# A gated recurrence with an MLP behind it: the fifth pair's q' and k' turned by the DMA crossbar, and loads that stop for other pairs than before

## The chip, the cores and the metric

One core of a Trainium2 chip runs the whole program. The metric is the device time of one execution in microseconds (us). The kernel before takes 172.65 us (median of three runs, 172.24 to 172.72). One more execution was profiled, and it took 172.37 us. Its span, from the first to the last recorded instruction, is 170.6 us, so 1.8 us lie outside the span.

## The reference

Two parts follow each other. The first is a gated linear recurrence over 4 batches, 8 heads, 768 steps and 48 features; the second is a two-layer MLP with a tanh GELU over all 3072 tokens.

```python
for t in range(S):
    state = alpha[:, :, t, :, None] * state + np.einsum('bhd,bhe->bhde', k[:, :, t], v[:, :, t])
    y[:, :, t] = np.einsum('bhd,bhde->bhe', q[:, :, t], state)
...
x = np.ascontiguousarray(attn_out.transpose(0, 2, 1, 3)).reshape(B * S, H * D)
h = x @ w_in
c = np.float32(np.sqrt(2.0 / np.pi))
g = 0.5 * h * (1.0 + np.tanh(c * (h + 0.044715 * h * h * h)))
return (g @ w_out).astype(np.float32)
```

w_in is 384 x 2048, w_out 2048 x 384. All inputs and the output are float32.

## The kernel before, in words

**Tiles.** The sequence is cut into six chunks of 128 steps. In a chunk the recurrence is done as attention with decays: from alpha come ln(alpha) (`ln`, ScalarE), its running sum (`cum`, a matmul with a triangle of ones), b = exp(sum) and 1/b (`b`, `binv`, ScalarE), and q' = q*b, k' = k/b (`qp`, `kp`, VectorE). Two batches of a chunk make a pair. There are twelve pairs, 0 to 11, so the fifth pair is number 4: pair m belongs to chunk m // 2.

**Turning.** The scores need q' and k' with features on the partitions. For pairs 0 to 4 of the kernel before TensorE turns them (`t`; for pairs 2, 3 and 4 that is `turn_halves`, 32 small transposes into PSUM) and VectorE or ScalarE copies the result to SBUF (`ev`, two copies of 128 x 1024). For the pairs in `TURN_QK` SyncE issues two crossbar DMAs instead (`turn_dma`, L423; `turn5.0` is q' of pair 5, `turn5.1` its k'), which write the turned tile `qkT` with no work on TensorE. In the same way x, the pair's result before the MLP, is turned by TensorE (`tx`, then the copy `xe`), or, for the pairs in `TURN_X`, by one crossbar DMA (`turn_x_dma`, L429; `turn6.2` is that of pair 6).

**The rest of a pair.** `attn` makes the scores and the part of y that comes from the state; `mask` (four on VectorE) zeroes what lies ahead; `y` adds the scores times v; `x` copies y out of PSUM; `kv` and `st` carry the state to the next chunk, with the chunk's last decay row turned by VectorE (`tr`, four per pair).

**The MLP.** A block is two batches of a chunk: `l120.0` to `l120.7` are the first layer of chunk 2, batches 0 and 1 (pair 4's x), six matmuls each; `gelu20.0` to `gelu20.7` follow on ScalarE; `l122` and `gelu22` are batches 2 and 3 (pair 5's x). `l220.0` to `l220.3` are the second layer of chunk 2, batch 0, four matmuls each, `ot20` copies the result out of PSUM, `store20` sends it. ScalarE needs one table for ln and exp and another for GELU; each change loads a table (1.28 us).

**Order.** Nothing is scheduled when the program is built: the list `FIRST` names every step with its engine (P TensorE, V VectorE, A ScalarE, G GpSimd, S SyncE), and each engine runs its own steps in the list's order and waits on semaphores.

**Loads.** q, k, v and alpha of later pairs come by DMAs that GpSimd issues (L246) in the order of `LOADS`. A `gate` (L254) is a one-element copy on GpSimd: it reads a byte of what it names and so holds everything behind it on GpSimd, loads and stores alike, until that has landed. `gate T 5 1` waits for the turned k' of pair 5, `gate X 6 0` for the turned x of pair 6, and from `window 3` on each load is also held until the load three before it has landed. Gates do not stop what is already in the DMA queues. Most stores of results go out from GpSimd too, the others from SyncE.

**Buffers that bind.** PSUM has four `ff` tiles (MLP, half of the scores), two `yk` tiles (turns, y, kv) and one `ca` tile (`cum`, the other half of the scores). Each is handed on when the copy or mask that reads it is done.

Of the kernel before, what the change touches and what calls it, by code (L numbers as in the profile page):

```python
# [76 lines left out]
class _Kernel:  # L77
# [5 lines left out]
             "aqkv 3", "aqkv 4", "aqkv 5", "aqk 6", "a 7", "gate T 5 1", "q 7", "a 8", "k 7", "v 6", "window 3", "v 7", "qkv 8", "gate T 6 0", "aq 9", "gate X 6 0", "kv 9", "aqkv 10", "a 11", "gate X 8 0", "qkv 11")  # L83
# [22 lines left out]
        P:l110.1 A:gelu10.5 V:ev3.0 A:ev3.1 P:kv2.1 P:l110.7 A:gelu10.3 A:gelu10.1 A:gelu10.7 P:kv3.0 V:tr3.2 V:tr3.3 V:st2.1 P:l110.4 A:gelu10.4
        P:l110.2 A:gelu10.2 P:l211.0 G:load.a7.0 V:st3.0 P:attn3.0 V:mask3.2 V:mask3.3 P:l211.1 P:l211.2 A:ln4.0 P:cum4.0 A:b4.0 V:mask3.0 V:mask3.1
        V:qp4.0 P:l210.0 P:y3.0 P:l211.3 A:x3.0 P:y3.1 P:kv3.1 A:binv4.0 P:l210.1 P:l210.2 V:st3.1 V:tr4.0 A:x3.1 A:ln5.0 P:tx3.1 V:xe3.1 A:ot11.0
        P:tx3.0 V:xe3.0 V:tr4.1 P:cum5.0 G:store02.0 A:b5.0 S:store03.0 P:l210.3 P:l112.0 P:l112.7 S:store11.0 A:ot10.0 A:binv5.0 V:kp4.0 V:qp5.0
        S:turn5.0 V:kp5.0 S:turn5.1 G:gate.T5.1 G:load.q7.0 G:load.a8.0 G:load.k7.0 G:load.v6.0 G:gate.a8.0 G:load.v7.0 A:gelu12.0 A:gelu12.7 P:t4.0  # L110
        V:ev4.0 P:l112.3 P:l112.5 V:ev4.1 V:tr4.2 V:tr4.3 P:l112.4 P:kv4.0 V:st4.0 A:gelu12.3 A:gelu12.5 A:gelu12.4 P:l112.6 A:gelu12.6 S:store01.0
        P:l112.1 P:l112.2 A:gelu12.1 V:tr5.0 P:attn4.0 A:gelu12.2 P:l212.0 P:l212.1 V:mask4.2 V:mask4.0 V:mask4.1 P:l212.2 P:y4.0 P:l212.3 V:mask4.3
        P:y4.1 A:ln6.0 P:cum6.0 A:x4.0 P:l213.0 V:tr5.1 A:ot12.0 A:x4.1 P:tx4.0 V:xe4.0 A:binv6.0 P:tx4.1 V:xe4.1 V:kp6.0 P:l213.1 A:b6.0 P:l213.2
        P:kv4.1 V:st4.1 P:l213.3 A:ln7.0 V:ot13.0 P:l120.0 P:attn5.0 V:mask5.0 V:mask5.1 V:mask5.2 V:mask5.3 V:tr6.0 V:tr6.2 V:tr6.1 P:l120.2 V:tr5.2
        V:tr5.3 A:gelu20.0 A:gelu20.2 P:l120.6 P:l120.7 A:gelu20.6 P:l120.1 A:gelu20.1 P:y5.0 V:x5.0 P:l120.4 A:gelu20.7 A:gelu20.4 P:l120.5 P:l120.3
        A:gelu20.5 V:qp6.0 V:tr6.3 G:gate.k7.0 G:load.q8.0 G:gate.v6.0 G:load.k8.0 S:turn6.1 A:gelu20.3 P:cum7.0 P:y5.1 V:x5.1 P:l221.0 P:kv5.0
        P:l220.0 P:tx5.1 P:l221.1 V:st5.0 G:gate.v7.0 G:load.v8.0 V:xe5.1 A:b7.0 P:l220.1 P:tx5.0 V:qp7.0 V:xe5.0 S:turn6.0 G:gate.T6.0 G:gate.q8.0
        G:load.a9.0 P:l221.2 P:kv5.1 A:binv7.0 S:turn7.0 V:st5.1 A:ln8.0 P:cum8.0 A:binv8.0 A:b8.0 P:l221.3 P:l220.2 P:l220.3 A:ot21.0 P:attn6.0
        V:kp7.0 A:ot20.0 P:l122.0 P:l122.2 G:store21.0 V:mask6.0 V:mask6.1 V:mask6.2 V:mask6.3 P:l122.7 A:gelu22.0 A:gelu22.2 P:l122.4 V:tr7.0 V:tr7.1
        G:store13.0 G:store12.0 P:y6.0 A:gelu22.4 A:gelu22.7 P:l122.1 P:y6.1 A:gelu22.1 A:x6.0 P:l122.6 V:x6.1 P:l122.3 G:store10.0 P:kv6.1 V:st6.1  # L120
        P:l122.5 P:kv6.0 V:st6.0 P:l223.0 A:gelu22.3 P:l223.1 A:gelu22.6 A:gelu22.5 P:l223.2 S:turn7.1 G:store20.0 S:turn6.2 G:gate.k8.0 V:qp8.0
# [22 lines left out]
    """.split()  # L144
    ACROSS, GAP = (0, 1), 112

    TURN_QK, TURN_X = (5, 6, 7, 8, 9, 10, 11), (6, 7, 8, 9, 10, 11)

    XPK = 48
    INTER = (2, 3, 4, 5, 6, 7, 8, 9, 10, 11)  # L150
# [9 lines left out]
                a=5, q=5, k=5, vb=5)  # L160
# [713 lines left out]
```

## Time and profile before

| | |
|---|---|
| median of three runs | 172.65 us (172.24 to 172.72) |
| profiled execution | 172.37 us, of it span 170.6 us |
| TensorE busy | 164.7 us (97%) |
| ScalarE busy | 127.0 us (74%) |
| VectorE busy | 105.5 us (62%) |
| GpSimd busy | 73.2 us (43%) |
| read from and written to memory | 25.17 MB and 4.72 MB |

How to read it: a matmul's record covers its way through the array, so that a busy TensorE overlaps itself. What a matmul costs is read from the distance between starts, which the chain of waits gives. Crossbar DMAs and loads are busy neither on SyncE nor on an engine; their cost is the time from issue to landing, and who waits for the landing. The row of a gate on GpSimd shows how long loads stood still.

### The profile page before, as it was taken

Reading aid. Unit: us, or ns where it says so; the run is one execution under the profiler, and the core shown is the slowest. Engines: PE = TensorE matmul, PEld = TensorE weight load, DVE = VectorE, ACT = ScalarE, POOL = GpSimd, SP = SyncE. Lnnn points to the kernel's source line nnn. Section 1 sums busy time; section 2 is a strip of 40 time slices with the busy share of each in tenths; the row PEclk is TensorE's granted clock in tenths of the full one; section 3 lists DMA queues with packets and bytes.
Section 4 is the critical chain, followed back from the end, with each engine's and each line's share of the span. In section 5 each row is a group of like instructions: output and inputs, shape, how many; then the busy total and the mean of one; then the engine's idle time right before and its main releaser. Section 6 shows DMA issues by size and latency. Waiting matters only on the chain.

```text
span 170.6 us, 4706 instructions
## 1 busy us (share of the span) xinstructions
PE 164.7 (97%) x1965; PEld 130.3 (76%) x1966; DVE 105.5 (62%) x201; ACT 127.0 (74%) x207; POOL 73.2 (43%) x100
## 2 busy tenths in 40 slices
PE   7799999999999999999999999999999999999993
PEld 2478899666886797796697697796796795986973
DVE  6499512478978997799877957765953740620000
ACT  3687688897998998969788399587978783453741
POOL 6488346996565003753990267350800600100000
PEclk9999999999999999999999999999999999999999
DMA  4999999999999995899999999999397595121104
GB/s 132 303 215 158 224 252 253 223 218 217 262 212 192 218 210 140 205 168 181 194 230 306 151 137 130 190 197 258 85 180 169 81 176 124 50 53 39 50 0 140
DMA packets 56389, 29.53 MB, mean 173 GB/s; under 512 B 45840, under 2 KB 52432, under 8 KB 56368
## 3 DMA queue, kind: packets, MB, share of 16 engines
q0 software_dynamic: 31216, 19.67, 71.0%
q1 hardware_dynamic: 24608, 9.18, 29.7%
q10 hardware_dynamic: 544, 0.39, 0.8%
q8 instruction: 15, 0.25, 0.6%
q14 instruction: 6, 0.05, 0.1%
HBM read 25.17 MB, written 4.72 MB: 175 GB/s over the span
## 4 chain that ended last, share of the span: by engine, by line
PE 81%; DMA 7%; DVE 4%; ACT 3%; SPq 2%; issue 1%; POOL 1%; POOLq 0%
PE hT L558 34%; PE acc L577 33%; DMA wide<-in_v_dram 4%; PE at L447 3%; DMA k<-in_k_dram 3%; PE yps L526 2%; PE cum L318 2%; PE kv L476 2%; DVE tr L490 2%; SPq L243 2%; DVE atm L466 1%; ACT qkT L386 1%; PE yps L456 1%; PE xT_ps L545 1%; PE xT_ps L516 1%
## 5 line engine op out<-in xcount | busy, mean ns | idle before, releaser
L558 PE MATMUL hT<-xT,w_in 128*128 128x256 bf16 (+1 forms) x672 | 69.9, 258 | 0.0
L577 PE MATMUL acc<-w_out,gT 128*128 128x384 bf16 (+3 forms) x416 | 68.6, 314 | 0.0
L564 ACT ACTIVATE gT<-hT 128x512 bf16<-128x512 f32 x96 | 52.6, 602 | 15.0 <-PE hT L558 13.9
L558 PEld LDWEIGHTS <-w_in 128*128 128x128 bf16 x672 | 61.9, 113 | 1.4
L577 PEld LDWEIGHTS <-gT 128*128 128x128 bf16 x416 | 37.3, 98 | 20.3
L466 DVE TENSOR_TENSOR atm<-at,ut 128x512 bf16<-128x512 f32 x48 | 30.2, 683 | 4.9 <-PE at L447 4.9
L589 DVE COPY ot<-acc 128x384 f32<-128x384 f32 (+1 forms) x7 | 3.6, 509 | 25.8 <-PE acc L577 25.6
L589 ACT COPY ot<-acc 128x384 f32<-128x384 f32 (+2 forms) x19 | 8.8, 461 | 13.4 <-PE acc L577 9.6
L602 POOL DMA_DIRECT2D out_dram<-ot x14 | 7.7, 553 | 19.9 <-DVE ot L589 19.7
L355 DVE TENSOR_TENSOR kp<-k,binv 128x768 bf16<-128x768 f32 (+1 forms) x15 | 11.9, 795 | 4.9 <-DMA k<-in_k_dram 2.2
L490 DVE STREAM_TRANSPOSE tr<-b 32x256 f32<-32x256 f32 x32 | 14.0, 439 | 0.8
L246 POOL DMA_DIRECT2D q<-in_q_dram x11 | 12.3, 1115 | 4.6 <-DMA w_in<-in_moe_w_in_dram 2.2
L246 POOL DMA_DIRECT2D a<-in_alpha_dram x11 | 12.2, 1110 | 4.2 <-issue 1.1
L218 ACT ACT_TABLE_LOAD x10 | 12.8, 1283 | 0.9 <-PEq L858 0.7
L246 POOL DMA_DIRECT2D k<-in_k_dram x11 | 12.2, 1113 | 2.8 <-issue 1.2
L501 DVE TENSOR_TENSOR stmp<-kv,st 128x384 f32<-128x384 f32 x16 | 8.9, 557 | 7.2 <-PE kv L476 6.5
L246 POOL DMA_DIRECT2D vb<-in_v_dram x11 | 12.2, 1108 | 2.3 <-issue 0.6
L564 ACT ACT_TABLE_LOAD x10 | 12.8, 1283 | 0.2
L355 DVE TENSOR_TENSOR qp<-q,b 128x768 bf16<-128x768 f32 (+1 forms) x15 | 11.9, 795 | 1.4 <-ACT b L344 1.2
L344 ACT ACTIVATE b<-cum 128x768 f32<-128x768 f32 (+1 forms) x15 | 10.1, 684 | 2.5 <-PE cum L318 1.5
L344 ACT ACTIVATE binv<-cum 128x768 bf16<-128x768 f32 (+1 forms) x15 | 10.3, 689 | 1.6 <-PE cum L318 1.4
L503 DVE TENSOR_TENSOR st<-stmp,tr 128x384 bf16<-128x384 f32 x16 | 8.9, 558 | 0.6
(77 smaller groups left out, 149.0 us busy)
## 6 DMA issues: line engine op xcount, KB each, us to landing
a<-in_alpha_dram POOLq DMA_DIRECT2D x9, 384.0 KB, 9.0
q<-in_q_dram POOLq DMA_DIRECT2D x9, 384.0 KB, 8.0
k<-in_k_dram POOLq DMA_DIRECT2D x9, 384.0 KB, 8.0
out_dram<-ot POOLq DMA_DIRECT2D x10, 192.0 KB, 6.3
vb<-in_v_dram POOLq DMA_DIRECT2D x9, 192.0 KB, 8.0
out_dram<-ot SPq DMA_DIRECT2D x9, 192.0 KB, 2.4
w_in<-in_moe_w_in_dram POOLq DMA_DIRECT2D x4, 384.0 KB, 8.5
w_out<-in_moe_w_out_dram POOLq DMA_DIRECT2D x4, 384.0 KB, 10.5
```

Of the source, the lines that this page charges most:

```text
L218: nc.scalar.add_instruction(mybir.InstLoadActFuncSet(name=nc.get_next_instruction_name(), act_func_set_id=i, engine=mybir.EngineType.Activ ...
L246: dma(u[t][:, lo:hi].rearrange("t b h d -> t (b h) d"), src.rearrange("b h s d -> s (b h) d")[c * C:(c + 1) * C])
L344: self.nc.scalar.activation(u[n].rearrange("t i h d -> t i (h d)")[:, lo:hi], cum, AF.Exp, scale=1.0 if n == "b" else -1.0)
L355: self.nc.vector.tensor_tensor(out, rows, b, op=ALU.mult)
L466: self.nc.vector.tensor_tensor(u["atm", i][:, o], u["at", i][o], self.ut[:, None, :].to_broadcast([self.C, self.H // 2, self.C]), op=ALU.mult)
L490: self.nc.vector.transpose(u["tr"][f:f + 32, :, 0:32], rows[:, lo:lo + H * 2 * D].rearrange("t (g n) -> t g n", n=2 * D)[:, :, 0:32])
L501: nc.vector.tensor_tensor(s, acc, old, op=ALU.add)
L503: nc.vector.tensor_tensor(new, acc, end[:, :, None].to_broadcast([C, H // 2, 2 * D]), op=ALU.mult)
L558: self.nc.tensor.matmul(h[:, s].rearrange("p (g t) -> p g t", t=self.C), w_in[:, j, nt % 4 + s], self.xT[c % self.NX][:, lo:hi, j], start= ...
L564: return lambda e: self.nc.scalar.activation(self.gT[c % self.NG][:, nt:nt + 4 // (hi - lo), lo * self.C:hi * self.C], f.pop(("h", c, lo, ...
L577: self.nc.tensor.matmul(f["acc", c, b][:, lo:hi], self.gT[c % self.NG][:, nt, b * self.C:(b + 1) * self.C], self.w_out[:, nt, lo:hi], star ...
L589: self.copy(e)(f["ot", c, b][:, sl], f["acc", c, b] if half is None else f["acc", c, b, half][:, sl])
```

## The change

`TURN_QK` gets pair 4, so that its q' and k' are turned by two crossbar DMAs (`turn4.1`, `turn4.0`). TensorE's `t4.0` (32 transposes) and the two copies `ev4.0` and `ev4.1` on VectorE go.

`LOADS` gets other gates and another order. Before there were T5 (k'), T6 (q'), X6 and X8. Now there are T4 (q'), T5 (q' and k'), T7 (q' and k'), X6 and X8: no gate for the turned q' of pair 6, two more stops for pairs 4 and 7.

`FIRST` is written anew. On each engine the order is the same as before up to the start of chunk 1's MLP (about 45 us into the span) and again from `l142` on (about 134 us); between, it differs on all five engines. No step other than those named is added or removed.

```diff
     LOADS = ("gate a 0 1", "v 0", "gate k 0 1", "in 0", "v 1", "in 1", "in 2", "in 3", "out 0", "out 1", "aqk 2 a", "out 2", "aqk 2 b", "out 3", "v 2",
-             "aqkv 3", "aqkv 4", "aqkv 5", "aqk 6", "a 7", "gate T 5 1", "q 7", "a 8", "k 7", "v 6", "window 3", "v 7", "qkv 8", "gate T 6 0", "aq 9", "gate X 6 0", "kv 9", "aqkv 10", "a 11", "gate X 8 0", "qkv 11")
+             "aqkv 3", "aqkv 4", "aqk 5", "a 6", "gate T 4 0", "k 6", "a 7", "q 6", "gate T 5 0", "gate T 5 1", "v 5", "q 7", "a 8", "k 7", "v 6", "window 3", "v 7", "q 8", "a 9", "gate T 7 0", "gate T 7 1", "gate X 6 0", "kv 8", "qkv 9", "aqkv 10", "a 11", "gate X 8 0", "qkv 11")
...
-        G:load.q9.0 G:gate.X6.0 P:l222.0 V:tr7.2 V:tr7.3 V:kp8.0 P:l222.1 S:turn8.0 P:attn7.0 V:mask7.2 V:mask7.3 P:l223.3 A:ln9.0 P:l222.2 P:l222.3
...
+        P:attn7.0 A:gelu22.1 A:gelu22.3 G:store21.0 G:store13.0 G:store12.0 G:store10.0 G:store20.0 S:turn6.2 G:gate.X6.0 G:gate.v7.0 G:load.k8.0
...
-    TURN_QK, TURN_X = (5, 6, 7, 8, 9, 10, 11), (6, 7, 8, 9, 10, 11)
+    TURN_QK, TURN_X = (4, 5, 6, 7, 8, 9, 10, 11), (6, 7, 8, 9, 10, 11)
```

GpSimd, from the load of pair 8's q to the gate X6 (`gate<-xT_103`), before the change. `gate<-qkT` is the gate T6, the other gates are those of the window; the loads of k and vb are pair 8's, those of a and of the second q pair 9's:

```order
L246 DMA q<-in_q_dram 128x16x48
L254 CAST gate<-vb 128x1
L246 DMA k<-in_k_dram 128x16x48
L254 CAST gate<-vb 128x1
L246 DMA vb<-in_v_dram 128x16x48
L254 CAST gate<-qkT 128x1
L254 COPY gate<-q 128x1
L246 DMA a<-in_alpha_dram 128x16x48
L602 DMA out_dram<-ot 128x384 x5
L254 COPY gate<-k 128x1
L246 DMA q<-in_q_dram 128x16x48
L254 CAST gate<-xT_103 128x1
```

The same engine from the load of pair 8's q on in the changed kernel. `gate<-qkT 128x1 x2` are the two gates T7, and k, vb and the second q behind `gate<-xT_103` are pair 8's k and v and pair 9's q:

```order
L247 DMA q<-in_q_dram 128x16x48
L255 CAST gate<-vb 128x1
L247 DMA a<-in_alpha_dram 128x16x48
L255 CAST gate<-qkT 128x1 x2
L603 DMA out_dram<-ot 128x384 x5
L255 CAST gate<-xT_103 128x1
L255 CAST gate<-vb 128x1
L247 DMA k<-in_k_dram 128x16x48
L255 COPY gate<-q 128x1
L247 DMA vb<-in_v_dram 128x16x48
L255 COPY gate<-a 128x1
L247 DMA q<-in_q_dram 128x16x48
```

Pair 8's k and v have moved from ahead of the five stores to behind them and behind the gate X6.

SyncE, from its first store to the turned q' of pair 7, in the changed kernel (`kp_95` and `qp_91` are k' and q' of pair 4; the rows behind the three stores are pairs 5, 6 and 7):

```order
L603 DMA out_dram<-ot 128x384
L424 DMA_TRANSPOSE qkT<-kp_95 128x8x128
L424 DMA_TRANSPOSE qkT<-qp_91 128x8x128
L603 DMA out_dram<-ot 128x384 x3
L424 DMA_TRANSPOSE qkT<-qp_92 128x8x128
L424 DMA_TRANSPOSE qkT<-kp_96 128x8x128
L424 DMA_TRANSPOSE qkT<-kp_97 128x8x128
L424 DMA_TRANSPOSE qkT<-qp_93 128x8x128
L424 DMA_TRANSPOSE qkT<-kp_98 128x8x128
L424 DMA_TRANSPOSE qkT<-qp_94 128x8x128
```

Before, the rows of `kp_95` and `qp_91` were not there, and the first crossbar DMA was pair 5's; now three stores and pair 5's two turns stand behind pair 4's two.

VectorE, from q' of pair 8 (`qp_91`), which stands behind the first of pair 7's four masks, to its k' (`kp_95`), in the changed kernel; `atm` are the other three masks, `tr` decay rows, `ot` the result of chunk 2's batch 3, the two `x` are pair 7's:

```order
L356 TENSOR_TENSOR qp_91<-q,b_99 128x16x48
L491 STREAM_TRANSPOSE tr<-b_100 32x8x32
L467 TENSOR_TENSOR atm<-at,ut 128x512
L491 STREAM_TRANSPOSE tr<-b_99 32x8x32
L467 TENSOR_TENSOR atm<-at,ut 128x512 x2
L590 COPY ot<-acc 128x384
L491 STREAM_TRANSPOSE tr<-b_99 32x8x32
L537 CAST x<-yps 128x8x48
L491 STREAM_TRANSPOSE tr<-b_99 32x8x32
L537 CAST x<-yps 128x8x48
L356 TENSOR_TENSOR kp_95<-k,binv 128x16x48
```

Before, k' of pair 8 stood ahead of the four masks of pair 7. On TensorE `l130.1`, a first user of pair 6's turned x, now stands one second-layer step behind `attn7.0`; before, `l130.0` was the first, three second-layer steps and `cum9.0` behind `attn7.0`.

More of the change, by code (lines that the diff above doesn't have):

```diff
@@ L106 @@
[L106 to L113, printed above, removed]
@@ L118 @@
[L118 to L121, printed above, removed]
```

95 lines of the change are left out of this document (54 added, 41 removed).

## The prediction, on record before the changed kernel ran

> **What bounds the kernel now.** I began with the page: busy times, the granted clock, the shares of the chain of waits.
>
> ```profile
> span 170.6 us, 4706 instructions
> ...
> PE 164.7 (97%) x1965; PEld 130.3 (76%) x1966; DVE 105.5 (62%) x201; ACT 127.0 (74%) x207; POOL 73.2 (43%) x100
> ...
> PEclk9999999999999999999999999999999999999999
> DMA  4999999999999995899999999999397595121104
> ...
> PE 81%; DMA 7%; DVE 4%; ACT 3%; SPq 2%; issue 1%; POOL 1%; POOLq 0%
> ```
>
> TensorE is the bound, at a full granted clock. The DMA engines are also occupied nearly throughout up to three quarters of the span, so whatever is added there must share. Then the chain of waits in order of time, which has what each step of TensorE costs:
>
> ```profile
> 59.05 0.57 PE qkT_ps L379 x32
> ...
> 63.98 0.55 PE at L447 x16
> 64.53 0.20 PE yps L456 x16
> ...
> 66.79 0.20 PE yps L526 x8
> 66.99 0.65 PE acc L577 x4
> ...
> 67.84 0.33 PE cum L318 x2
> ...
> 70.45 0.17 PE kv L476 x4
> 70.62 0.65 PE acc L577 x4
> 71.27 0.65 PE hT L558 x6
> ```
>
> A step of either MLP layer costs 0.65 us, the scores 0.75, a `y` 0.20, a `cum` 0.33, a `kv` 0.17. From 45 us to the end these fill TensorE almost without a hole, and what stands in the list behind 134 us is the same in both kernels. So only two things can move the end: work that leaves TensorE, and waits of TensorE that go or come between 45 and 134 us.
>
> **What goes.** `t4.0` takes 0.57 us (first row above); with the 0.1 us that TensorE loses when it turns to 64-row matmuls (60 us less the step ahead of it, below) that is **0.67 us**.
>
> ```profile
> 51.27 1.48 PE L577 MATMUL acc<-w_out,gT 128*128 128x384 bf16 x8
> 52.77 0.48 PE L318 MATMUL cum<-la,ut_h 128*128 128x384 f16 x2
> ...
> 57.58 1.47 PE L558 MATMUL hT<-xT,w_in 128*128 128x256 bf16 x12
> 58.98 0.41 PE L379 MATMUL qkT_ps<-ident,qp 64*128 64x64 bf16 x16
> ...
> 78.78 0.81 PE L577 MATMUL acc<-w_out,gT 128*128 128x384 bf16 x4
> 79.76 0.34 PE L545 MATMUL xT_ps<-ident,x 128*128 128x128 bf16 x3 [0.16 <-DVE x L536]
> ```
>
> Two steps from 57.58 would end at 58.88, and the transposes start at 58.98: the 0.1 us. The same subtraction gives the waits that stand there now: 52.77 - 51.27 - 1.30 = 0.20 us ahead of pair 4's `cum`, and 79.76 - 78.78 - 0.65 = 0.33 us ahead of pair 5's `tx`. In the new order one step of the MLP more stands ahead of `cum4.0`, and `x5.1` is read 2.6 us later, behind four second-layer steps, so I let both go: **0.53 us**. VectorE is also rid of two copies (0.69 us each, as another pair's copy below shows); it is not the bound, so this counts only through the waits.
>
> ```profile
> 46.23 0.69 DVE L386 COPY qkT<-qkT_ps 128x1024 bf16<-128x1024 bf16 x1
> ...
> 64.02 0.60 ACT L564 ACTIVATE gT<-hT 128x512 bf16<-128x512 f32 x1
> 64.63 1.28 ACT L218 ACT_TABLE_LOAD   x1
> 65.93 0.84 ACT L301 ACTIVATE la<-a 128x768 f16<-128x768 f32 x1
> ...
> 84.59 0.62 PE L447 MATMUL at<-qkT 64*128 64x128 bf16 x16
> ...
> 85.02 2.48 DVE L466 TENSOR_TENSOR atm<-at,ut 128x512 bf16<-128x512 f32 x4 [0.58 <-PE at L447]
> ...
> 89.25 0.56 DVE L536 CAST x<-yps 128x384 bf16<-128x384 f32 x1 [0.82 <-PE yps L526]
> ...
> 94.98 0.96 DVE L355 TENSOR_TENSOR kp<-k,binv 128x768 bf16<-128x768 f32 x1
> ```
>
> **Short waits that come.** Positions in the new order come from the step costs above, laid along the new list from 45 us on. Pair 4's scores begin at 63.4 (63.98 less `t4.0`'s 0.67, less the 0.20, plus a wait of 0.2 below and small change). With TensorE that much ahead, ScalarE's pace shows. The last GELU of `l112` ends about 64.3 (64.62 in its row, 0.3 earlier now), then the table (1.28) and ln of pair 6 (0.84) end at 66.5; `cum6.0` is due at 66.3 (scores 63.4 + 0.75, three steps, one `y`): 0.2. In the same way `cum8.0` waits 0.1, `l211.0` 0.2 (on ScalarE the copy `ev3.0` stands ahead of `gelu10.1`). The masks of pair 6 stand behind three small VectorE steps and end 0.3 after `y6.1` is due; `ot23.0` behind pair 7's masks frees its PSUM tile 0.25 late for `l130.3`; `y8.1` waits 0.1. Together **1.2 us**. None of these exists in the trace of before; each is a handover that I know to about 0.2 us, so the sum lies between 0.3 and 2.0.
>
> **What the added crossbar DMAs cost.** First the microseconds from issue to landing: of all turned q' and k', of `turn6.2` (answer for 90 to 91 us), of pair 9's k and pair 8's k' (97 to 99 us), and the median of GpSimd's stores. Then the issues on SyncE and GpSimd, a gate, and the first user of `turn6.2` on TensorE, in the timeline:
>
> ```profile
> DMA to landing us min/median/max: 2.7/5.6/7.7
> ...
> xT<-x SPq DMA_TRANSPOSE x1, 6.5
> ...
> k<-in_k_dram POOLq DMA_DIRECT2D x1, 384.0 KB, 5.7
> ...
> qkT<-kp SPq DMA_TRANSPOSE x1, 2.7
> ...
> out_dram<-ot POOLq DMA_DIRECT2D x10, 192.0 KB, 6.3
> ```
>
> ```profile
> 90.16 2.10 SPq L429 DMA_TRANSPOSE xT<-x  x1
> ...
> 79.05 1.16 POOL L246 DMA_DIRECT2D k<-in_k_dram  x1 [0.37 <-DVE qp L355]
> ...
> 85.58 2.71 POOL L602 DMA_DIRECT2D out_dram<-ot  x5
> ...
> 96.74 0.18 POOL L254 CAST gate<-xT 128x1 f32<-128x1 bf16 x1 [7.16 <-DMA xT<-x]
> ...
> 97.37 1.17 POOL L246 DMA_DIRECT2D k<-in_k_dram  x1 [0.19 <-issue]
> ...
> 97.75 0.82 PE L558 MATMUL hT<-xT,w_in 128*128 128x256 bf16 x6
> ```
>
> A turned q' or k' takes 2.7 to 7.7 us to land; the shortest is pair 8's k', issued while GpSimd stood still (the 7.16 us in front of X6). For pair 4 the new writes are issued at about 55.0 and 56.5 (k' and q' behind pair 3's masks) and read at 63.4: 6.9 us for the later one. With the loads stopped behind pair 6's alpha I take no wait; without that cover it is at most 0.8 (7.7 - 6.9). Pair 5's are read at 71, pair 6's q' is issued at 76.5 and read at 84.4: 7.9 us, no wait. Behind pair 5's gate stands pair 5's v, needed at 75.0; the gate opens at about 65, so it lands in time. The three stores that now stand behind pair 4's turns on SyncE keep nobody waiting.
>
> The price lies between the scores of pairs 6 and 8. **First, x of pair 6.** VectorE ended its masks 0.43 + 2.48 = 2.9 us after the start of `attn6.0`; three small steps stand ahead of them now, so 3.2. Two copies of 0.56 follow, and `turn6.2` is issued at 4.35. TensorE has until `l130.1` eight steps of `l122`, two `y`, two `kv`, `attn7.0` and `l223.0`, with the scores at the start 0.75 + 5.24 + 0.41 + 0.34 + 0.85 + 0.65, and the wait of 0.3 above: 8.55. So 4.2 us are left, where before it was 97.75 - 90.16 = 7.6 us, and the write took 6.5 of them. Alone it takes about 3 (pair 8's 2.7); but the five stores, freed when pair 7's gate opens (its second write issued at 84.3, behind `kp7.0`, so about 87.5), go out in the same microseconds, as they did before (85.58 on), and loads do not. I take 4.8, between: a wait of **0.6**, bounds 0 (2.7) and 2.3 (6.5).
>
> **Second, k' of pair 8.** Its load was issued at 79.05; now it stands behind X6. From the issue of `turn6.2`: landing 4.8, gate and issue 0.6 (96.74 to 97.37), load 5.7, `kp8.0` 1.0: `turn8.1` is issued at 12.1. The loads behind are running again, so I take 6.2 to land, in the upper half of the row: 18.3. TensorE needs from `l130.1` to the scores of pair 8 eight first-layer and ten second-layer steps, two `y`, a `cum`, two `kv` and the short wait: 13.1, so 4.8 + 13.1 = 17.9. A wait of **0.4**, bounds 0 and 3.0 (if both writes take longest). VectorE is not held for it: behind `kp8.0` stands `st7.1`, whose `kv` comes later. Pair 9's loads start some 3 us later than before, and are read that much later too.
>
> **Sum.** -0.67 - 0.53 + 1.2 + 0.6 + 0.4 = +1.0 us. The profiled execution took 172.37 us (span 170.6 and 1.8 around it), so 173.4; the median of the runs shown is 0.28 above that execution, which gives **173.6 us**.
>
> [...]
>
> **Rivals.**
>
> *The stops do what they can, and TensorE is never kept.* Place: the 4.2 us of `turn6.2` and the 5.8 left for `turn8.1`. For it speaks that pair 8's k', with GpSimd held, took 2.7 us, and that VectorE starts 1.4 us lighter. Both waits are then 0, and if the short waits are half of my sum the result is -1.2 + 0.6 = -0.6: **172.0 us**, faster. It decides at 4.2 us for `turn6.2`.
>
> *The stores hold x.* The stop for pair 7 releases five stores immediately ahead of `turn6.2`; such stores land 6.3 us after issue (last row). If the turned x lands only with the last of them, at 87.5 + 2.7 + 6.3 = 96.5, against 92.9 due, TensorE waits 3.6 and k of pair 8 follows later still: 173.6 + 3.0 = **176.6 us**. Against it: SyncE's queue is another one than GpSimd's. [...]
>
> *Pair 4's turns are late.* The loads ahead of T4 are still in the queues, and with 7.7 us and a second delay on pair 5's gate `attn4.0` and `y5.0` wait together some 2 us: **175.5 us**. For it: the loads that are in the queues there took 11 to 12 us to land (answer for 44 to 53.5 us, pair 5's and 6's k).
>
> ```profile
> k<-in_k_dram POOLq DMA_DIRECT2D x2, 384.0 KB, 11.8
> ```
>
> *Given back exactly:* one of the two waits, fewer short ones, within 0.3% of before, about **172.7 us**.
>
> **How the numbers follow.** Forecast (0.3 to 2.2 us above before) 0.45; never kept 0.22; stores hold x 0.13; pair 4 late 0.08; given back 0.12. A measurement of this kernel tells about 0.3% (0.5 us) from no change. Faster by more than that: most of the second case, 0.19. Within: the last case, the rest of the second and the lower end of the forecast, 0.21. Slower: 0.60. The range goes from 171.6 (172.65 - 1.2 + short waits of 0.3, and 0.15 for the scatter of runs) to 176.2, which leaves out most of the stores' case and a tail below.
>
> **What would show it.** In the changed profile: 32 matmuls of L379 fewer, and no hole in TensorE at 52.8 and 79.8; a hole in TensorE ahead of the first `hT` behind the seventh scores, ended by the DMA of x, and one ahead of pair 8's scores, ended by the DMA of k'; the gate X6 opening at 93 to 95; the loads of pair 8's k landing near 100. If TensorE has no hole there, the waits were wrong; if holes stand before 80 us, pair 4 or 5 was late; if the short waits in front of the `cum` steps are absent, ScalarE was not as close behind as I say.

## The result, and the profile after

The changed kernel takes **176.7 us** (median of five runs, 175.9 to 177.75); the kernel before took 172.33 us beside it (five runs, 171.81 to 172.72). The ratio is 1.0258, with a 95% interval from 1.0211 to 1.0305. The prediction had the sign right and the size wrong: +4.4 us where it said +1.0, and outside its range. The profiled execution of the changed kernel took 176.54 us, of it span 174.7. (Medians here are over all runs of a kernel; ratios leave disturbed runs out, so the two need not match exactly.)

First the page of the changed kernel: the span, TensorE, the DMA engines by slices of 4.37 us, the chain by engine, k' on VectorE, and the gates on turned q' and k'.

```profile
span 174.7 us, 4655 instructions
...
PE 165.2 (95%) x1933; PEld 130.4 (75%) x1934; DVE 105.6 (60%) x202; ACT 126.5 (72%) x204; POOL 74.9 (43%) x105
...
DMA  4999999999994889999994999999994494121104
...
PE 63%; DMA 23%; ACT 5%; POOL 4%; issue 2%; SPq 1%; DVE 1%; POOLq 0%; ACTq 0%
...
L356 DVE TENSOR_TENSOR kp<-k,binv 128x768 bf16<-128x768 f32 (+1 forms) x15 | 11.9, 795 | 6.5 <-DMA k<-in_k_dram 5.3
...
L255 POOL CAST gate<-qkT 128x1 f32<-128x1 bf16 x5 | 1.6, 323 | 26.5 <-DMA qkT<-qp 24.0
```

TensorE is as busy as before; what is new is that the chain runs 23% of the span through DMAs (7% before) and that VectorE waits 5.3 us for k (2.2 before). The row of the DMA engines has two slices at 4 that were full before, from 52 to 57 us and from 92 to 96 us: there the loads stood still at a gate. GpSimd waited 26.5 us in front of turned q' and k' (12.2 before).

Then TensorE in the timeline (start, duration, step; the bracket is the idle time before the row), at the places that the prediction named:

```profile
51.73 1.47 PE L578 MATMUL acc<-w_out,gT 128*128 128x384 bf16 x8
53.24 0.48 PE L319 MATMUL cum<-la,ut_h 128*128 128x384 f16 x2
...
66.41 0.36 PE L527 MATMUL yps<-vb,atm 128*128 128x48 bf16 x8
66.77 0.48 PE L319 MATMUL cum<-la,ut_h 128*128 128x384 f16 x2
...
81.19 0.81 PE L578 MATMUL acc<-w_out,gT 128*128 128x384 bf16 x4
81.99 0.48 PE L319 MATMUL cum<-la,ut_h 128*128 128x384 f16 x2
...
90.30 1.25 PE L559 MATMUL hT<-xT,w_in 128*128 128x256 bf16 x10
92.25 0.62 PE L448 MATMUL at<-qkT 64*128 64x128 bf16 x16 [0.70 <-ACT gT L565]
...
93.66 0.82 PE L559 MATMUL hT<-xT,w_in 128*128 128x256 bf16 x6
...
104.20 2.44 PE L578 MATMUL acc<-w_out,gT 128*128 128x384 bf16 x14
109.26 0.62 PE L448 MATMUL at<-qkT 64*128 64x128 bf16 x16 [2.62 <-DMA qkT<-kp]
```

Distances between starts give the holes, as in the prediction: ten first-layer matmuls at 0.109 us end at 91.39 and pair 7's scores start at 92.25, a hole of 0.86; fourteen second-layer matmuls at 0.163 end at 106.48 and pair 8's scores start at 109.26, a hole of 2.78. (The bracket shows 0.16 us less each time: a matmul's record is that much longer than the distance between starts, 0.273 us against 0.109 in the first layer, 0.326 against 0.163 in the second.) Of each hole 0.10 us is not new: TensorE lost that ahead of these scores in the kernel before too (109.06 - 103.76 - 5.20 for pair 8, with 5.20 for 32 second-layer matmuls). `cum4.0` still waits 0.20, `cum6.0` 0.16, `cum8.0` 0.15; `y6.1` waits 0.24, a first-layer step at 128.8 waits 0.33, and `kv3.0` at 49.41 now waits 0.17. The bracket at 92.25 names a GELU, but that is not who was waited for: in the experiment e7 the same GELU ends at 92.39 and the scores stand at 91.69. Pair 7's turned q' landed at 92.11, as the chain shows.

The chain of waits of the changed kernel from 84 to 110 us (start, duration, what):

```profile
84.50 7.61 DMA qkT<-qp
...
92.48 0.18 POOL gate L255
...
93.04 1.38 POOL out_dram L603 x3
...
95.77 0.20 POOL gate L255
...
96.39 6.44 DMA k<-in_k_dram
...
102.85 0.96 DVE kp L356
...
103.84 5.38 DMA qkT<-kp
...
109.26 0.62 PE at L448 x16
```

These eight rows carry most of the loss. Pair 7's q' takes 7.61 us to land. Until then its gate holds GpSimd, behind it five stores have to be issued, then comes the gate X6 (no wait any more), and only at 96.39 the load of pair 8's k; 6.44 later VectorE makes k', 5.38 after that it is turned, and TensorE, which asked at 106.48, goes on at 109.26.

The stops that stand ahead of all this are those for pairs 4 and 5, in GpSimd's timeline of the changed kernel:

```profile
61.62 0.18 POOL L255 CAST gate<-qkT 128x1 f32<-128x1 bf16 x1 [15.09 <-DMA qkT<-qp]
...
68.40 0.86 POOL L255 CAST gate<-qkT 128x1 f32<-128x1 bf16 x1 [2.45 <-DMA qkT<-kp]
```

They hold the loads for 15.1 and 2.5 us, and v of pair 7 is issued at 79.5. In the kernel before the one stop here held them for 12.0 us, and v of pair 7 went out at 74.1.

The account closes. At `l142.0`, behind which both lists are the same, the changed kernel is 3.76 us later. The profiled run was 0.30 later already at pair 2's scores (37.81 against 37.51), where the lists are still the same. Then -0.67 (`t4.0`), -0.33 (pair 5's `tx`), +0.17 (`kv3.0`), +0.55 (`cum6.0`, `cum8.0`, `y6.1`), +0.76 and +2.68 (the two holes less their 0.10 each) and +0.33 make 3.79.

### The profile page after: what moved, and what is told of

Same layout as the page of the kernel before. It is cut to its first block, busy times and chain, and to the rows that moved or that the text cites. A ratio compares the mean times of both kernels' runs of the same rounds, so it can differ in the third digit from the quotient of the medians.

```text
span 174.7 us, 4655 instructions
## 1 busy us (share of the span) xinstructions
PE 165.2 (95%) x1933; PEld 130.4 (75%) x1934; DVE 105.6 (60%) x202; ACT 126.5 (72%) x204; POOL 74.9 (43%) x105
## 4 chain that ended last, share of the span: by engine, by line
PE 63%; DMA 23%; ACT 5%; POOL 4%; issue 2%; SPq 1%; DVE 1%; POOLq 0%; ACTq 0%
PE acc L578 26%; PE hT L559 26%; DMA k<-in_k_dram 7%; DMA qkT<-qp 4%; DMA wide<-in_v_dram 4%; DMA out_dram<-ot 4%; DMA qkT<-kp 3%; PE at L448 2%; PE cum L319 2%; PE yps L527 2%; PE kv L477 2%; POOL out_dram L603 2%; SPq L244 1%; ACT L565 1%; ACT qkT L387 1%
## 5 line engine op out<-in xcount | busy, mean ns | idle before, releaser
L590 ACT COPY ot<-acc 128x384 f32<-128x384 f32 (+2 forms) x18 | 8.3, 459 | 14.3 <-PE acc L578 9.3
L603 POOL DMA_DIRECT2D out_dram<-ot x16 | 8.8, 554 | 21.2 <-DVE ot L590 19.3
L247 POOL DMA_DIRECT2D a<-in_alpha_dram x11 | 12.2, 1111 | 3.9 <-issue 1.6
L247 POOL DMA_DIRECT2D q<-in_q_dram x11 | 12.2, 1112 | 2.2 <-DMA w_in<-in_moe_w_in_dram 1.0
L247 POOL DMA_DIRECT2D vb<-in_v_dram x11 | 12.2, 1111 | 2.2 <-DMA w_out<-in_moe_w_out_dram 1.1
L255 POOL CAST gate<-qkT 128x1 f32<-128x1 bf16 x5 | 1.6, 323 | 26.5 <-DMA qkT<-qp 24.0
```

The source lines that it names most:

```text
L247: dma(u[t][:, lo:hi].rearrange("t b h d -> t (b h) d"), src.rearrange("b h s d -> s (b h) d")[c * C:(c + 1) * C])
L590: self.copy(e)(f["ot", c, b][:, sl], f["acc", c, b] if half is None else f["acc", c, b, half][:, sl])
L603: return lambda e: (self.nc.sync if e == "SP" else self.nc.gpsimd).dma_start(self.out[r:r + self.C, sl], f["ot", c, b][:, sl])
```

## The experiments

Each kernel was timed against the kernel before on the same chip, which took 172.04 to 172.18 us there. The first theory, from the trace above, was **L**: what the stops take from the loads makes later loads land late, and TensorE waits where its list meets them. Its narrow form is that only pair 8's k, behind pair 7's stop, is late. The rival **S**: the crossbar's own writes are slow whatever the loads do.

### e1: is the late k of pair 8 the loss?

```diff
+            mine = self.p[3, 1] if (u["m"], n) == (8, "k") else u
-            out, rows, b = u[n + "p"][:, lo:hi, :, 0:self.D], u[n][:, lo:hi], u["b" if n == "q" else "binv"][:, lo:hi]
+            out, rows, b = u[n + "p"][:, lo:hi, :, 0:self.D], mine[n][:, lo:hi], u["b" if n == "q" else "binv"][:, lo:hi]
```

> The changed kernel, but k' of pair 8 is made from pair 7's k, which is long there; pair 8's k is still loaded and never read, so the result is not the reference's. Theory 'late load': the 2.8 us hole of TensorE ahead of pair 8's scores is the late k of pair 8. VectorE then makes k' at about 100.4 instead of 102.9, the crossbar write is issued about 2.5 us earlier, the hole shrinks to 0.3 to 0.5, and the time falls by about 2.3 us, to about 174.4. Rival 'slow write': the hole is the crossbar write's own length among running loads; it starts earlier, meets more loads, still lands near 109, and the time stays within 0.7 us of 176.7.

Measured: 176.72 us, ratio 1.0244 (1.0187 to 1.0301), no gain. TensorE of e1 in the timeline:

```profile
92.07 0.62 PE L448 MATMUL at<-qkT 64*128 64x128 bf16 x16 [1.31 <-DMA qkT<-qp]
107.73 0.62 PE L448 MATMUL at<-qkT 64*128 64x128 bf16 x16 [1.27 <-DMA qkT<-kp]
126.91 2.12 PE L559 MATMUL hT<-xT,w_in 128*128 128x256 bf16 x18 [1.77 <-ACT ot L590]
129.56 0.81 PE L559 MATMUL hT<-xT,w_in 128*128 128x256 bf16 x6 [0.53 <-ACT gT L565]
```

k' of pair 8 was made at 100.2 instead of 102.85 and the hole ahead of pair 8's scores halved, but the one ahead of pair 7's scores grew to 1.48, and new ones opened in chunk 4's first layer. There ScalarE's copy of a result (`ot`) had waited 2.76 us for an earlier store to land (126.28), and the matmuls wait for what ScalarE does then; the 0.33 of the change at 128.8 has the same cause (a store that lands at 125.51). The narrow form falls: without the late k the time stays, and the waits stand elsewhere.

### e2, e3: one stop fewer

e2 takes `gate T 4 0` out of `LOADS`, e3 both `gate T 7`; nothing else.

> The changed kernel without the gate on the turned q' of pair 4: GpSimd goes on loading k, alpha, q at 47 us instead of 62. Theory 'lost load time': the 15 us during which GpSimd stood still put every later load about 4 us behind the old order; without this stop q, alpha, k of pairs 7 and 8 land 3 to 4 us earlier, the loads ahead of pair 7's stop have drained when its crossbar writes are issued, that stop opens at about 88 instead of 92, k of pair 8 lands at about 98, and both holes (0.9 and 2.8 us) go: about 173.3. Against it stands that pair 4's own crossbar writes then share with loads and land 2 to 4 us later than at 61.6, against 63.7 due: up to 2 us are lost there, so 173.3 to 175. Theory 'late load' alone, with pair 7's stop as the cause, leaves the stop opening above 91 and the time within 0.7 us of 176.7.

Measured: 177.74 us, ratio 1.0292 (1.0222 to 1.0363). TensorE of e2 in the timeline (of a run of 181.31 us, the longest of four):

```profile
64.52 0.62 PE L447 MATMUL at<-qkT 64*128 64x128 bf16 x16 [1.95 <-DMA qkT<-qp]
94.91 0.62 PE L447 MATMUL at<-qkT 64*128 64x128 bf16 x16 [1.05 <-DMA qkT<-qp]
112.38 0.62 PE L447 MATMUL at<-qkT 64*128 64x128 bf16 x16 [3.07 <-DMA qkT<-kp]
```

Without the stop pair 4's turned q' itself comes late, and the two later holes stay. No load time came back: pair 5's turns stand behind pair 4's on SyncE, GpSimd stood 15.6 us at pair 5's gate instead, and v of pair 7 went out at 80.4. So e2 does not test the lost load time. It does show that, once pair 4 goes by the crossbar, pair 4's own scores wait if its stop is taken out.

> The changed kernel without the two gates on pair 7. Theory 'late load': GpSimd issues the five stores at 83 instead of 93 and then stands at the gate on x of pair 6, whose write is now slower (stores beside it): it lands at 94 to 96, k of pair 8 is issued at about the same time as now (96.4) or 1.5 us earlier; the hole ahead of pair 8's scores shrinks by no more than 1.5 us, and one of 1 to 2 us opens ahead of the first user of x: 175.5 to 177.5. Rival 'pair 7's stop is the whole cost': with it gone the time returns to 173 to 174.

Measured: 177.33 us, ratio 1.0203 (1.0146 to 1.0259). TensorE of e3 in the timeline:

```profile
92.14 0.62 PE L447 MATMUL at<-qkT 64*128 64x128 bf16 x16 [0.48 <-DMA qkT<-qp]
94.60 0.85 PE L558 MATMUL hT<-xT,w_in 128*128 128x256 bf16 x6 [0.89 <-DMA xT<-x]
108.74 0.62 PE L447 MATMUL at<-qkT 64*128 64x128 bf16 x16 [1.13 <-DMA qkT<-kp]
```

The hole at pair 8 shrinks, x of pair 6 is now late for `l130.1`. The interval overlaps the change's: no verdict between the two on the time, only on the places. The rival's 173 to 174 us falls: by the ratio it is 175.5.

### e4: pair 4 by the crossbar in the kernel before

Only `TURN_QK` with pair 4 and `turn4.0`, `turn4.1` behind `kp4.0`; no new stop, no new order.

> The kernel before with one part of the change alone: q' and k' of pair 4 go by the crossbar, directly behind k' of pair 4 on SyncE's list; no gate, no load and no other step is moved. Theory: the two writes meet a queue with 11 us of loads, land not before 65, and TensorE waits 1.5 to 3 us ahead of pair 4's scores, less the 0.7 that leave it: 173.3 to 174.8. If a crossbar write is as quick among loads as alone (3 to 4 us), it lands by 63 and the time is 171.7 to 172.2.

Measured: 176.63 us, ratio 1.018 (1.0092 to 1.0267). Pair 4's turn is late by 2.44 us at 65.58, and that hole has an after-effect (under e8). Taking 0.67 us of transposes off TensorE costs more than it brings here too.

### e5: no loads from pair 8 on

```diff
+            if u["m"] > 7:
+                u[t] = self.p[3, 1][t]
+                return
```

> The changed kernel without the loads of a, q, k and v of pairs 8 to 11: their tiles stand for pair 7's, so part of the output is computed from pair 7's inputs; every stop, transpose, matmul and store stays. Theory L (the stops take load time out of DMA queues that were nearly always busy, so that the loads of pairs 7 to 11 land 5 to 17 us later and TensorE meets them): nothing of pairs 8 to 11 is late any more, turn8.1 is issued near 95 and takes under 4 us, the holes ahead of attn7 (0.86 us), attn8 (2.78 us) and l140.2 (0.33 us) go, and the time is 172.0 to 173.2 us. Rival S (the crossbar writes themselves, 5 to 8 us each, are what is late, whatever the loads do): turn7.0 and turn8.1 still take 5 us and more, at least 2 us of the holes stay, and the time is 175 us or more.

Measured: 175.12 us (173.28 to 176.24), ratio 1.0138 (1.0027 to 1.0248): the median is S's number, the interval also holds L's. The places speak against S: turn7.0 landed in 2.8 us and turn8.1 in 3.4, and the holes ahead of both scores went. But another came, 2.2 us ahead of `l130.1`, in TensorE's timeline of e5:

```profile
94.64 1.47 PE L561 MATMUL hT<-xT,w_in 128*128 128x256 bf16 x6 [2.06 <-DMA xT<-x]
```

Pair 7's gate opened at 86.90, so the five stores went out beside `turn6.2`, which took 6.3 us. That looks like the prediction's rival "the stores hold x", seen here once. In e7, with the gate at 87.80, it took 3.7 us beside the same five stores and nothing waited. Two of the stores were issued ahead of it in e5 (6.3 us), one in e7 and e10 (3.7 and 4.3), none in e9 (2.7), which fits the rival. No run varies the stores alone, so the cause is not shown.

### e6: the old loads from pair 7 on, behind the stops for pairs 4 and 5

```diff
-... "v 7", "q 8", "a 9", "gate T 7 0", "gate T 7 1", "gate X 6 0", "kv 8", "qkv 9", ...
+... "v 7", "qkv 8", "gate T 6 0", "aq 9", "gate X 6 0", "kv 9", ...
```

> The changed kernel with the kernel before's list of loads from v of pair 7 on: no stop for pair 7, k and v of pair 8 ahead of a of pair 9, the stop for q' of pair 6 back; the stops for pairs 4 and 5 and everything else stay. Theory L: k of pair 8 is issued near 84 and lands near 90 (5 us behind the kernel before, 12 us ahead of the change), kp8 near 96 to 98, the hole ahead of attn8 falls under 1 us, but what the stops for pairs 4 and 5 took is still missing, so that 1 to 2 us of waits show elsewhere: 173.5 to 175.5 us. Rival S: turn7 and turn8.1 run among loads and take longer, 176.5 us or more. If the stop for pair 7 alone made all of the loss: 172.0 to 173.0 us.

Measured: 177.96 us, ratio 1.0274 (1.0167 to 1.0381), again the number of S. TensorE of e6 in the timeline:

```profile
96.97 1.47 PE L558 MATMUL hT<-xT,w_in 128*128 128x256 bf16 x6 [4.78 <-DMA xT<-x]
```

Pair 8's k is early now (landed 89.7), but x of pair 6 takes 9.3 us among the running loads (4.3 in the change), and its first user, which the new order has 4 us earlier (93.66 in the change, 97.75 before), waits 4.9. Neither theory had this place. So with the old loads the new order loses here without the stop for pair 7 (in e3, which has no such stop either but keeps pair 8's k behind the gate X6, the wait is 1.05).

### e7: pair 4 by TensorE again

```diff
-    TURN_QK, TURN_X = (4, 5, 6, 7, 8, 9, 10, 11), (6, 7, 8, 9, 10, 11)
+    TURN_QK, TURN_X = (5, 6, 7, 8, 9, 10, 11), (6, 7, 8, 9, 10, 11)
...
-... "a 6", "gate T 4 0", "k 6", ...
+... "a 6", "k 6", ...
```

with `t4.0`, `ev4.0` and `ev4.1` ahead of `kv4.0`.

> The changed kernel with pair 4's q', k' turned by TensorE again (eight transposes and two evictions) and without the stop for them; the stops for pairs 5 and 7, the new order and the later place of k of pair 8 stay. Theory L: the loads up to pair 7 regain about 3 to 5 us, turn7 lands 3 us or more earlier, the gate of pair 7 opens near 88 to 89 as the prediction had it, k of pair 8 lands near 99, the holes ahead of attn7 and attn8 shrink from 3.6 to under 1.5 us; the transposes cost 0.7 us: 173.5 to 175.0 us. If the place of k of pair 8 behind pair 7's stop alone decides, the hole ahead of attn8 stays over 2 us and the time is 176.5 us or more.

Measured: **173.48 us** (ten runs), ratio 1.0094 (1.0056 to 1.0132). GpSimd of e7 in the timeline:

```profile
79.66 1.16 POOL L246 DMA_DIRECT2D a<-in_alpha_dram  x1 [0.46 <-issue]
87.80 0.43 POOL L254 CAST gate<-qkT 128x1 f32<-128x1 bf16 x2 [6.98 <-DMA qkT<-qp]
88.61 2.71 POOL L602 DMA_DIRECT2D out_dram<-ot  x5 [0.37 <-ACT gT L564]
92.55 0.18 POOL L254 CAST gate<-xT 128x1 f32<-128x1 bf16 x1 [1.23 <-DMA xT<-x]
...
93.42 1.18 POOL L246 DMA_DIRECT2D k<-in_k_dram  x1 [0.44 <-issue]
```

Pair 7's q', issued at the same time as in the change (84.7), lands in 3.0 us instead of 7.6, the gate opens at 87.80, pair 8's k is issued 3 us earlier; no hole ahead of pair 7, 0.42 ahead of pair 8. Pair 4's part (its crossbar turns and the stop for them), which was to bring 0.67 us, costs 2.8 us by the ratios (1.0258 against 1.0094).

### e8: e4 with eight idle matmuls in the hole

> The kernel with only pair 4's transposes moved to the crossbar (no new stops, no new order), with eight idle 128x512 matmuls ahead of pair 4's attention, so that TensorE works through most of the 2.44 us in which it waited there. If the half clock that followed that hole (3.41 us at 0.5) comes from TensorE's having been idle: no half clock, mean granted clock 1.0, about 1.7 us less than without the fill, 174.2 to 175.2 us. If it has another cause (the crossbar's traffic, power): half clock stays, 176 us or more.

Measured: 175.36 us, ratio 1.0186 (1.0108 to 1.0264). The windows of both kernels, e4 first (from:to, length, busy times, then the granted clock PEclk, DMA share, GB/s):

```profile
63.00:66.00 3.00, 0.72 (x19) 0.46 (x19) 0.00 (x0) 2.91 (x4) 0.00 (x0) 1.00 1.14 225
66.00:69.40 3.40, 3.40 (x34) 1.79 (x29) 2.92 (x5) 0.09 (x1) 1.21 (x2) 0.51 0.51 135
69.40:76.00 6.60, 6.60 (x91) 4.72 (x90) 3.61 (x7) 5.37 (x8) 3.90 (x6) 1.00 0.96 189
```

The same stretch of e8:

```profile
63.00:66.00 3.00, 2.35 (x14) 1.19 (x12) 0.37 (x1) 2.91 (x5) 0.00 (x0) 1.00 1.24 174
66.00:69.40 3.40, 3.05 (x53) 2.20 (x54) 2.39 (x4) 0.47 (x1) 0.69 (x2) 1.00 0.73 185
```

In e4 TensorE worked 0.72 of the 3 us before 66, and the next 3.4 us went by at half clock; in e8 it was kept at work for 2.35, and the clock stayed at 1.00. From pair 4's scores to `cum6.0` e4 takes 5.36 us (65.58 to 70.94), e8 3.76 (66.35 to 70.11): 1.6 us. The whole time gained less, since the turned k' landed later in that run; the intervals overlap. Over the four runs of each, the mean granted clock was 0.99, 0.988, 0.99 and 1.0 in e4, and 1.0, 0.997, 1.0 and 0.999 in e8 (3.4 us at half clock make 0.99). Shown is the cause of the half clock, not the gain.

### e9, e12: the stop without the crossbar, and the lost load time without it

e9 is e7 with a stop put back: `"a 6", "gate T 4 1", "k 6"`, which opens when pair 4's transposes have been evicted.

> The kernel of e7_pair4_by_tensore (pair 4's q', k' by TensorE, 173.48 us) with a stop of the loads put back at the same place, without the crossbar transposes of pair 4: GpSimd waits there until TensorE's transposes of pair 4 have been evicted (near 60.4, in the change 61.6). Theory L2 (the lost load time behind pair 4's stop is the loss): loads from k of pair 6 on come 3 to 5 us later than in e7, turn7 runs among the loads v 7, q 8, a 9 again and takes over 5 us instead of 3.0, pair 7's gate opens at 90 or later instead of 87.8, k of pair 8 lands after 101, the hole ahead of attn8 is over 1.5 us (0.42 in e7): 175 to 176.5 us. Rival C (pair 4's crossbar transfers themselves hold the queues): as e7 within 0.7 us, 173 to 174.2 us.

Measured: 173.89 us, ratio 1.0089 (1.0053 to 1.0125), the number of rival C. But the stop took no load time: it opened at 59.7, pair 5's turns, now without loads beside them, landed in 2.7 to 2.8 us, and its gate opened at 64.4 (e7: 64.0, the change: 68.4); v of pair 7 was issued at 76.5 (75.4, 79.5). So it did not test L2, and e12 adds the missing time with one more gate, on k' of pair 6:

```diff
-... "gate T 5 0", "gate T 5 1", "v 5", ...
+... "gate T 5 0", "gate T 5 1", "gate K 6 0", "v 5", ...
```

> The kernel of e9_stop_without_crossbar (pair 4 by TensorE, a stop in its place, 173.89 us) with one more stop of the loads, behind pair 5's: GpSimd waits until k' of pair 6 is made (near 69.2), so that v of pair 5 and all behind it are issued when the change issues them (v of pair 5 at 69.2 there), and no crossbar transpose is added. Theory L2 (the loss of pair 4's part is the load time behind it): v of pair 7 is issued near 79.5 instead of 75.4 to 76.5, turn7 runs among v 7, q 8, a 9 and takes 6 us or more, pair 7's gate opens at 91 or later, the holes are near 0.9 us ahead of attn7 and 2.5 us ahead of attn8: 175.8 to 177.2 us. Rival C (what pair 4's crossbar transfers hold besides): within 0.7 us of e9, 173.2 to 174.6 us.

Measured: **177.76 us**, ratio 1.0298 (1.0243 to 1.0352). GpSimd of e12 in the timeline:

```profile
79.39 1.16 POOL L246 DMA_DIRECT2D vb<-in_v_dram  x1
...
82.60 1.16 POOL L246 DMA_DIRECT2D a<-in_alpha_dram  x1
93.06 0.43 POOL L254 CAST gate<-qkT 128x1 f32<-128x1 bf16 x2 [9.30 <-DMA qkT<-qp]
```

And TensorE of e12:

```profile
93.07 0.99 PE L447 MATMUL at<-qkT 64*128 64x128 bf16 x16 [2.13 <-DMA qkT<-qp]
...
109.95 0.62 PE L447 MATMUL at<-qkT 64*128 64x128 bf16 x16 [0.91 <-DMA qkT<-kp]
```

With pair 4 on TensorE and no added crossbar DMA, only v of pair 5 and what follows issued as late as in the change (69.2), everything is there again: v of pair 7 goes out at 79.39, pair 7's q' takes 9.1 us, its gate opens at 93.06, the holes stand at pairs 7 and 8. Rival C falls: late loads without pair 4's crossbar DMAs give a loss of the change's size. (It is divided otherwise: the hole ahead of pair 7 is longer than in the change and the one ahead of pair 8 shorter, and in the profiled run a half clock of 3.4 us follows the first; a run with a granted clock of 1.0 took 178.06 us.)

### e10, e11: the place of pair 8's k, and the new order alone

e10 is e7 with `"qk 8", "a 9", "gate T 7 0", "gate T 7 1", "gate X 6 0", "v 8"`.

> The kernel of e7_pair4_by_tensore with k of pair 8 ahead of a of pair 9 and of pair 7's stop. If the remaining 0.4 us hole ahead of attn8 and the 1 us of holes at pair 10's layer norm in e7 come from k and v of pair 8 standing behind pair 7's stop: both shrink, 172.3 to 173.0 us. If k of pair 8 ahead of the stop makes turn7 run among more loads (over 5 us instead of 3.0), attn7 waits instead: 174 us or more.

(What this text calls a layer norm is `ln`, the logarithm of alpha.) Measured: 173.49 us (twelve runs), ratio 1.0043 (1.0008 to 1.0078). By the ratio that is 172.9 us, the upper end of the first case: pair 7's turns stay short (3.0 us) and the holes in chunk 4's first layer go, but ahead of pair 8's scores 0.89 us stay, now because `turn8.1` takes 6.0 us among loads. It is the best of the variants and still not faster than before.

e11 is e7 with the kernel before's `LOADS`: the new order of the engines, without the stop for pair 7.

> The changed kernel's new order of TensorE, VectorE and ScalarE alone: pair 4 by TensorE, the loads and stops in the kernel before's order (no stop for pairs 4 and 7). By the prediction's sum the new order lets go 0.5 us of waits and adds up to 1.2 us of short ones; TensorE asks for attn8 near 106.4 and for l130.1 near 92 instead of 109 and 100. Theory L2: without pair 7's stop turn6.2 runs among loads and lands 95 to 97, so that l130.1, which the new order has 6 us earlier, waits 2 to 4 us: 174.5 to 176.5 us. If the order is harmless by itself: 171.7 to 173.0 us.

Measured: 179.6 us over six runs (175.92 to 182.9), ratio 1.028 (1.0206 to 1.0354). By the ratio that is 176.9 us, the first case or a little more. The chain of waits of e11, from a run of 180.88 us:

```profile
89.75 9.72 DMA xT<-x
...
99.51 1.47 PE hT L558 x6
```

X of pair 6 is under way for 9.72 us, and `l130.1` is 5.09 us late. The waits that the order lets go (0.33 us in the change) do not weigh against what it asks for early.

### e13: more work ahead of pair 8's scores

e10 with `l222.3` and `l231.0` (1.3 us) moved ahead of `attn8.0`.

> The kernel of e10_k8_early_no_pair4 (fast runs 1.0043 of the kernel before) with 1.3 us of TensorE work that stood behind pair 8's attention (two groups of the second matmul) put ahead of it. If the 0.89 us hole there is lost time by itself, it goes and nothing else moves: 0.6 to 0.9 us less than e10, a ratio of 0.998 to 1.002. If the hole is where the late loads happen to be met, it comes up again at the next demand (attn9, pair 10's layer norm): a ratio of 1.004 or more.

Measured: 175.51 us, ratio 1.016 (1.0098 to 1.0222). The hole went, but the moved work had covered VectorE's masks of pair 8, and `y8` now waits for these, as TensorE's timeline of e13 shows:

```profile
109.27 0.27 PE L526 MATMUL yps<-vb,atm 128*128 128x48 bf16 x4 [0.33 <-DVE atm L466]
109.87 0.27 PE L526 MATMUL yps<-vb,atm 128*128 128x48 bf16 x4 [0.33 <-DVE atm L466]
```

The profiled run, at 173.55, does not explain the others (up to 177.69 at full clock). The question put to it stays open, since the move made a wait of its own.

### Side by side

From the traces, in us; holes are distances between starts as above (the 0.10 us that stands ahead of all scores is left in a hole and alone counts as 0), X marks a step that the kernel doesn't have.

| | v 7 issued | turn7.0 issue > landing | pair 7's gate opens | turn6.2 takes | hole at l130.1 | at attn7 | at attn8 | ratio |
|---|---|---|---|---|---|---|---|---|
| before | 74.1 | 82.1 > 86.9 | X | 6.5 | 0 | 0 | 0 | 1 |
| the change | 79.5 | 84.5 > 92.1 | 92.2 | 4.3 | 0 | 0.86 | 2.78 | 1.0258 |
| e12 | 79.4 | 83.9 > 92.9 | 93.1 | 5.5 | 0 | 2.29 | 1.07 | 1.0298 |
| e9 | 76.5 | 84.5 > 88.7 | 88.8 | 2.7 | 0 | 0 | 1.18 | 1.0089 |
| e7 | 75.4 | 84.7 > 87.7 | 87.8 | 3.7 | 0 | 0 | 0.42 | 1.0094 |
| e10 | 74.5 | 84.7 > 87.8 | 87.9 | 4.3 | 0 | 0 | 0.89 | 1.0043 |
| e6 | 78.8 | 83.6 > 90.5 | X | 9.3 | 4.94 | 0.16 | 1.00 | 1.0274 |
| e11 | 74.5 | 85.7 > 92.9 | X | 9.7 | 5.09 | 0.42 | 0.40 | 1.028 |

The first column sets the second: where v of pair 7 goes out by 76.5 and pair 7's stop holds what follows, the turned q' lands in 3.0 to 4.2 us; at 79.4 and later it runs among v 7, q 8 and a 9 and takes 7.6 to 9.1.

## Why the prediction failed

**The step that failed** is "Second, k' of pair 8", priced at 0.4 and measured at 2.78 (2.68 of it new). Its demand side was right: TensorE was to ask 17.9 us after the issue of `turn6.2` (88.55), that is at 106.45, and asked at 106.48. The supply side was to come at 18.3 and came at 20.7 (109.22). Term by term: the load of pair 8's k was to be issued 5.4 us after `turn6.2` and was issued 7.84 after it (96.39), +2.44; the load took 6.44 instead of 5.7, +0.74; the turn took 5.38 instead of 6.2, -0.82.

The 2.44 come from one number in the step before: pair 7's gate was to open at "about 87.5", and opened at 92.23. The prediction let pair 7's q' land about 3 us after its issue at 84.3, as if no load were in flight beside it, and gave no time at which v of pair 7, q of pair 8 and a of pair 9 would go out. It priced the stops for pairs 4 and 5 only for who waits behind them directly (pair 5's v). The term for load time that is lost and not made up was missing from the sum. e7 shows the working to be sound where little of it is lost (gate 87.80), e12 that late loads without pair 4's crossbar DMAs make a loss of this size. The first slip can be seen at pair 5: its gate was to open "at about 65" and opened at 68.40, since its turned k' ran beside the loads that pair 4's gate had let go and took 5.7 us. Pair 5's v landed at 74.39, just in time for 75.20; in e3 it landed at 75.41, and TensorE waited 0.78.

The upper bound of 3.0 for this step does not come out of the prediction's own figures: with both writes at their longest the turned k' lands at 6.5 + 0.6 + 5.7 + 1.0 + 7.7 = 21.5 and is asked for at 6.5 + 13.1 = 19.6, a wait of 1.9. The measured wait lies above that.

**attn7, taken as free**: 0.86 (0.76 new), by the same late landing.

**First, x of pair 6** (0.6): measured 0. The landing was 4.3 against 4.8 assumed and 4.2 of slack, and the 0.86 lost just ahead covered what was left. The stores could not be beside it, as the gate had not let them go before 92.23: that the wait was small is luck, since the late gate that cost 2.78 at pair 8 kept them away here. e5, with the early gate that the prediction had assumed, has a wait of 2.2 at this place (the rival had 3.6).

**What goes**: `t4.0` right (0.67). Of the 0.53 of waits, `tx5`'s 0.33 went, `cum4.0`'s 0.20 stayed. **Short waits** (1.2): 0.55 came, at `cum6.0`, `cum8.0` and `y6.1`, 0.16, 0.15 and 0.24 against 0.2, 0.1 and 0.3; those at `l211.0`, `l130.3` and `y8.1` did not. One of 0.17 came that was not foreseen, at `kv3.0`, which starts 0.05 us after VectorE's copy `ev3.1` ends (49.36).

From +1.0 to the 3.46 measured behind the start: +2.28 (k' of pair 8, 2.68 against 0.4), +0.76 (attn7), +0.33 (chunk 4's first layer), +0.20 (`cum4.0`), +0.17 (`kv3.0`), -0.60 (x of pair 6), -0.65 (short waits). That is +2.49, so 3.49.

**The rivals**: "pair 4 late" and "never kept" did not happen in the change (`attn4.0` had no hole), but e2 and e4 show what would have made the former true. The rival that was missing is a stop whose price is paid some 30 us later (pair 4's gate opens at 61.6, the first hole begins at 91.4), at another pair's turn.

**What keeps e7 and e10 above the kernel before**, without a crossbar for pair 4, is in their traces. Behind their start (pair 2's scores) they reach pair 10's scores 1.80 and 1.38 us later than before. The short waits of the new order are larger here, and most of the 1.2 that the prediction had for them: `kv3.0` 0.16, `cum6.0` 0.36, `cum8.0` 0.15 and `y6.1` 0.23 make 0.90 in e10 (0.94 in e7). With 0.79 new at pair 8's scores, less the 0.33 of pair 5's `tx` that went, e10 has 1.36; with 0.32 there and 0.96 in chunk 4's first layer, less 0.33, e7 has 1.89. Open is why their runs scatter more than those of before.

## What to carry to other kernels

A stop of the loads is a debit on the DMA queues: here stops of 15.1 and 2.5 us, where one of 12.0 had stood, sent v of pair 7 out 5.4 us later (79.5 against 74.1), and pair 7's turned q' took 7.6 us instead of 4.8. Where the queues were busy nearly throughout, add up what each stop takes, carry the later times to every transfer behind it, and price the next crossbar write by what is in flight beside it at its new time, not at the old one. An order that asks for data earlier, and the stops that get it there, have to be summed as one; the order without the stops lost here too (e11, 1.028).

## What the hardware showed beyond that

**A crossbar write of the same size takes 2.7 to 9.1 us by its neighbours.** With the loads stopped, a turned q' or k' (128 x 1024 bf16, 256 KB) landed 2.7 us after issue for pair 8's k' in the kernel before, 2.8 for pair 7's q' in e5 and 3.0 in e7. Among loads pair 7's q' took 7.6 in the change and 9.1 in e12; pair 6's turned x (128 x 768) took 3.7 in e7 and 9.7 in e11. With the loads stopped this is not much more than a plain DMA takes here (in the change a stored result of 192 KB lands in 2.2 us right behind the stop); and the loads beside the slow writes (v 7, q 8 and a 9 in the change and e12) took 4.9 to 8.4 us themselves. So what counted in these runs is what else was in the queues.

**A short hole can halve TensorE's clock.** In the profiled runs seven holes of 2.1 to 5.1 us (two in e2, one each in e4, e5, e6, e11, e12) went with a stretch of about 3.4 us at a granted clock of 0.50, some 1.7 us lost each (half of 3.4); it began between 0.4 us before TensorE's return (e6, e11) and 1.1 us after it (e2). No hole under 2 us did this (the longest, 1.94 us in e1, stands in windows with a clock of 1.00), and the change's hole of 2.78 did not either: the twelve second-layer matmuls behind it took 1.96 us, 0.163 each as elsewhere. In the 3.4 us that end where the clock falls, TensorE was busy for 1.46 and 1.01 us in e2, 1.13 in e4, 1.35 in e5, 1.28 in e12 and not at all in e6 and e11. So the length of a hole alone does not tell: in e2 one of 2.1 us went with a fall, in the change one of 2.78 did not. What else decides is not shown.
